# Chunk members made later, block fetches and row scatters placed earlier, a wider token row: one change to a fused attention and mixture-of-experts kernel

## The chip, the cores and the metric

The kernel runs on one core of a Trainium2 chip. The metric is the device time of one execution in microseconds (us), the median of the runs. A core has five engines that work side by side, each through its own instructions in order: TensorE (PE; its weight loads are listed apart as PEld), VectorE (DVE), ScalarE (ACT), GpSimd (POOL) and SyncE (SP). SP issues most of the transfers, POOL those that cast or go by an index.

## The reference

```python
ub = sum(maximum(q * k_min[chunk], q * k_max[chunk]), axis=-1)      # a bound for each chunk of 32 keys
top_chunks = argsort(where(causal, ub, -1e9))[..., -6:]             # six chunks for each query
scores = where(key in a top chunk and key <= query, q @ k.T / sqrt(D), -1e9)
x = (softmax(scores) @ v).transpose(0, 2, 1, 3).reshape(3072, 512)

y_dense = relu(x @ w1_dense) @ w2_dense
expert = argmax(x @ w_gate, axis=1)                                 # one of 8
y_moe[t] = gate_w[t] * (relu(x[t] @ w1[expert[t]]) @ w2[expert[t]])
out = y_dense + y_moe
```

There are 4 batches, 8 heads, 768 positions and a head size of 64.

## The kernel before

**Attention.** The 32 heads are worked off as 16 pairs (`NP`), four pairs to a batch; a pair has 11 units (`u`), each of one score tile (`scores`), its exponential on ACT (L558), in three of the 11 units a causal mask on POOL (L560), and one unit later the product with v (`av`, L573). A pair is prepared ahead: POOL casts k, q and v to 16 bits (`cast_qk`, `cast_v`), PE transposes them (`prep_k`, `prep_q`), ACT and DVE evict them, DVE reduces each chunk to its maximum and minimum (L496), PE makes the bounds (`prep_ub`, L527), DVE finds the six largest (L533) and the flags, and `prep_s` brings the flags into the upper or lower half of the queries' tile `rT`. The keys' tile `kT` carries beside the 64 numbers of a key the row of chunk members: `exf` has -30000 where a key is in a chunk and 0 elsewhere, made by two selects on POOL (L135, L137) and copied by `expand` into the six `kT` tiles on ACT (L145, L146). So one matmul gives the scores and shuts out what was not chosen.

**Dense part and routing.** When a batch's four pairs are done, `batch_fills` hangs its dense layers and its routing between the units of the next four pairs; the table `at` says at which unit: transposes (L267), gate, `ranks` (L296), and `place(t)` for six tiles of 128 tokens. `place` is an indirect transfer by POOL (L378) that scatters tokens into a table in HBM, sorted by expert. A row has the 512 numbers of x, the gate's weight and the token's number, `XW` = 528 elements of 2 bytes. `xbig` has two buffers, so the copy of the token numbers (L292, POOL) for a batch waits for the scatters of the batch two before.

**Expert part.** The table is worked off in blocks of 128 rows. `lists` makes each block's expert offset (`eo`) and row (`ro`); `load_rows` and `load_offs` bring them into registers of SP and PE through `registers` (L440, TENSOR_LOAD), `fetch` (L459) loads a block by its register, `tx` transposes it (L686), `e1` and `th` and `e2` are the two layers, and an indirect add (L715) sends the result to the output. The first `N1` = 11 blocks hold no token of the last batch, so they can be fetched before that batch is routed. 28 blocks run in the loop; three more run only if they are needed. `empty` writes zero rows behind each expert's tokens (L730).

**What sets the order.** The program's order is written out by hand, and a scheduler may move an instruction against its neighbours on an engine; each engine then works strictly in its order and waits on semaphores. SP's queue holds the loads, the stores of dense results (L408), the register loads and the fetches one behind the other. The token numbers' copy, the casts, the masks, the scatters and the weights' loads (`load_expert`, L207) share POOL's queue.

Of the kernel before, what the change touches and what calls it, by code (L numbers as in the profile page):

```python
# [12 lines left out]
ALU = mybir.AluOpType  # L13
# [4 lines left out]
def kernel(  # L18
# [22 lines left out]
    HP = H // 2  # L41
    NP = B * HP
    NBLK = NM + E - 1
    XW = Dm + 16
    U16 = mybir.dt.uint16

    const = ctx.enter_context(tc.tile_pool(name="const", bufs=1))
# [31 lines left out]
    def load(p, names="kqv"):  # L79
        if p >= NP:  # L80
            return
        b, hp = divmod(p, HP)
        for nm, src in (("k", k), ("q", q), ("v", v)):
            if nm not in names:
                continue
            f = aload.tile([128, 2, NT, D], FP, name=nm + "f")
            st[p][nm] = f
            for g in range(2):
                if nm == "v":
                    nc.sync.dma_start(out=f[:, g], in_=src[b, 2 * hp + g].rearrange("(t p) d -> p t d", p=128))  # L90
                else:
                    nc.sync.dma_start(out=f[:, g].rearrange("p (T j) d -> p T (j d)", j=NJ),
                                      in_=src[b, 2 * hp + g].rearrange("(T p j) d -> p T (j d)", p=128, j=NJ))
# [37 lines left out]
    for j in range(NJ):  # L131
        cb = cbias[64 * j : 64 * j + 64]
        nc.gpsimd.affine_select(out=cb, in_=cb, compare_op=ALU.is_ge,
                                fill=-60000.0, base=j, pattern=[[128, NT], [0, 2], [-32, NC]], channel_multiplier=2)
    nc.gpsimd.affine_select(out=exf[0:32], in_=exf[0:32], compare_op=ALU.is_ge, fill=0.0,  # L135
                            base=0, pattern=[[1, S]], channel_multiplier=-32)
    nc.gpsimd.affine_select(out=exf[0:32], in_=exf[0:32], compare_op=ALU.is_ge, fill=0.0,  # L137
                            base=31, pattern=[[-1, S]], channel_multiplier=32)
    for i in range(NB):
        nc.vector.memset(kT[i][0][64:128], 0.0)  # L140
        nc.vector.memset(kT[i][1][0:64], 0.0)
        nc.vector.memset(v16[i][:, :, :, D : D + 1], 1.0)

    def expand(i):
        nc.scalar.copy(kT[i][0][64:96, :], exf[0:32])  # L145
        nc.scalar.copy(kT[i][1][0:32, :], exf[0:32])  # L146
# [111 lines left out]
    def batch_fills(b):  # L258
# [111 lines left out]
        def place(t):  # L370

            def f():
                with tc.issue_after(latest["pool"].ins):
                    put(t)
            return f
# [51 lines left out]
            at.setdefault(n + n // NT, []).append(f)  # L427
        at.setdefault(9, []).append(ranks)
        for t in range(NT):
            at.setdefault(11 + 5 * t, []).append(place(t))  # L430
        U = HP * NU
        for n, f in enumerate(dense):
            at.setdefault(10 + n * (U - 12) // len(dense), []).append(f)
# [4 lines left out]

    def registers(src, engine, top, why):
        _, v = nc.values_load_multi_w_load_instructions(src, engines=[engine], min_val=0, max_val=top,  # L440
                                                        skip_runtime_bounds_check_because=why)
        return v

    def load_offs():
# [12 lines left out]
    def fetch(i):  # L457
        es[i]["x"] = xg = eg.tile([128, XW], U16, name="xg")
        ld = nc.sync.dma_start(out=xg, in_=table[bass.ds(rows[i], 128)])  # L459
        if i < N1:  # L460
            tc.add_to_no_dep_group("full", ld.ins)

    FIRST = 6
    with (
# [7 lines left out]
        def cast_qk(p):  # L472
            if p >= NP:
                return
            s = st[p]
            s["k16"] = k16 = ahead.tile([128, NT, 2, D], HF, name="k16")
            nc.gpsimd.tensor_copy(k16, s["k"].rearrange("p g t d -> p t g d"))  # L477
            s["q16"] = q16 = ahead.tile([128, NT, 2, D], HF, name="q16")
            nc.gpsimd.tensor_copy(q16, s["q"].rearrange("p g t d -> p t g d"))
# [39 lines left out]
        def prep_ub(p):  # L519

            s = st[p]
            ub = pprep.tile([128, NT, 2, NC], FP, name="pp")
            nc.tensor.matmul(ub.rearrange("p t g c -> p (t g c)"), ident, cbias.rearrange("p t g c -> p (t g c)"),
                             start=True, stop=False, skip_group_check=True)
            for t in range(NT):
                for n, (src, j) in enumerate(((s["qp"], 0), (s["qp"], 2), (rT[p % NB][0], 1))):
                    nc.tensor.matmul(ub[:, t].rearrange("p g c -> p (g c)"), src[:, t * 128 : (t + 1) * 128],  # L527
                                     s["kb"][:, j].rearrange("p g c -> p (g c)"),
                                     start=False, stop=(n == 2), skip_group_check=True)
            m = m8[p % 2]  # L530
            for t in range(1, NT):
                for g in range(2):
                    nc.vector.max(out=m[:, t, g], in_=ub[:, t, g, 0 : 4 * t + 4])  # L533
            flags = fl[p % 2].rearrange("p t (g c) -> p t g c", g=2)[:, :, :, 0:NC]
            nc.vector.tensor_tensor(flags, ub, m[:, :, :, 5:6].to_broadcast([128, NT, 2, NC]), ALU.is_lt)
# [50 lines left out]

        for kind in ("tr", "h", "y", "rk"):
            cur[kind] = (pfill, "fb")
        for i in range(NB):
            expand(i)  # L590
        cast_qk(0)
        load(2, "kq")
        prep_k(0)
        prep_q(0)
        prep_kt(0)
        cast_v(0)
        prep_ub(0)
        cast_qk(1)
        load(3, "kq")
        cast_v(1)  # L600
# [5 lines left out]
        prep_kt(1)  # L606
        cast_qk(2)
        load(4, "kq")
        prep_ub(1)

        wq = [(e, w) for e in range(E) for w in range(2)]
        ahead_n = 2
# [15 lines left out]
        for i, (p, u) in enumerate(seq):  # L628
            n1 = p + 1 if p + 1 < NP else None
            n2 = p + 2 if p + 2 < NP else None  # L630
            if i + ahead_n < len(seq):
                scores(*seq[i + ahead_n])
            if u == 2 and n1 is not None:
                prep_s(n1)
            if u == 4 and n2 is not None:
                prep_k(n2)
            if u == 5 and n2 is not None:
                prep_q(n2)
            if u == 7 and n2 is not None:
                prep_kt(n2)  # L640
            if u == 9 and n2 is not None:
                prep_ub(n2)
            for f in fills.pop(i % (HP * NU) - LAG, ()):
                f()
            if i >= LAG:
                finish(*seq[i - LAG])
            if u == 0 and n2 is not None:
                cast_v(n2)
                load(p + 4, "v")
                if p == 1:  # L650
                    load_dense(st[n2]["cast"])
                if p == 2:
                    route_consts()
                for _ in range(2 if p >= 10 else 1):
                    if p > 1 and wq:
                        load_expert(*wq.pop(0), st[n2]["cast"])
            if u == 7:
                cast_qk(p + 3)
                load(p + 5, "kq")
            if p == NP - 1 and u == 5:  # L660
                load_rows(N1)
                load_offs()
            if p == NP - 1 and u >= 5:
                fetch(u - 5)
        for i in range(len(seq) - LAG, len(seq)):
            finish(*seq[i])
        assert not wq
# [133 lines left out]
```

## Time and profile before

| | |
|---|---|
| median of 3 runs | 273.51 us (273.25 to 274.56) |
| the profiled execution: span, and its own time | 273.5 us, 275.16 us |
| busy: PE, DVE, ACT, POOL | 219.3 us (80%), 189.2 us (69%), 170.8 us (62%), 159.2 us (58%) |
| longest groups | exponentials (ACT, L558) 91.0 us; scores (PE, L554) 63.5 us; products with v (PE, L573) 45.7 us |
| transfers | 49.64 MB, mean 182 GB/s |
| granted clock of TensorE, mean | 0.985 |

The shares are means over stages of different kinds: attention up to about 179 us, with dense work hung in from the fifth pair on, then expert blocks with the last batch's dense part, and a tail of adds. Each stage has to be read by itself. A wait is told with the engine or transfer that ended it; a wait for several is put down to the last one.

### The profile page before, as it was taken

How to read it: one execution, taken by the hardware profiler on the slowest of the kernel's cores; microseconds unless marked ns; L12 is line 12 of the kernel's file. 1: busy time of each engine (PE TensorE's matmuls, PEld its weight loads, DVE VectorE, ACT ScalarE, POOL GpSimd, SP SyncE). 2: the span in 40 equal slices, each digit the busy share in tenths (PEclk: the TensorE clock that was granted, in tenths of full speed). 3: DMA queues.
4: the chain of work that ended last, by engine and by line, in shares of the span. 5: the costliest groups of instructions: out<-in, count | busy, mean ns of one | idle time of the engine just before them, and what ended most of it. 6: DMA issues, size and time to landing. Idle time of an engine off the chain costs nothing. (4 is left out here: it accounts for less than half of the span.)

```text
span 273.5 us, 7279 instructions
## 1 busy us (share of the span) xinstructions
PE 219.3 (80%) x2547; PEld 144.5 (53%) x2547; DVE 189.2 (69%) x587; ACT 170.8 (62%) x319; POOL 159.2 (58%) x197
## 2 busy tenths in 40 slices
PE   1159777888898968899995899939968999999970
PEld 0147565666565656656664666616524555555530
DVE  6288999999989759998797997216634345545540
ACT  2819979778669858668987568813424555555530
POOL 7565976546567656576827534400783445776662
PEclk9999999999999999999999999998999999999996
DMA  6999999998979989879996924256396999886875
GB/s 178 268 255 275 162 235 184 237 225 208 194 178 287 200 257 232 164 191 188 213 250 121 186 78 109 62 163 159 89 297 100 258 170 238 143 139 89 100 102 75
DMA packets 75108, 49.64 MB, mean 182 GB/s; under 512 B 29632, under 2 KB 68160, under 8 KB 75072
## 3 DMA queue, kind: packets, MB, share of 16 engines
q1 hardware_dynamic: 59856, 30.18, 43.7%
q0 software_dynamic: 15216, 18.99, 43.0%
q8 instruction: 21, 0.34, 0.5%
q14 instruction: 15, 0.12, 0.2%
HBM read 41.55 MB, written 18.09 MB: 218 GB/s over the span
## 5 line engine op out<-in xcount | busy, mean ns | idle before, releaser
L558 ACT ACTIVATE ex<-sp 128x512 f16<-128x512 f32 (+1 forms) x176 | 91.0, 595 | 17.7 <-PE sp L554 11.7
L554 PE MATMUL sp<-rT,kT 128*128 128x128 f16 (+3 forms) x384 | 63.5, 261 | 5.9 <-ACT ex L558 4.1
L715 POOL DMA_INDIRECT out_dram<-yo,xg x28 | 43.7, 1561 | 24.9 <-DVE yo L714 17.0
L573 PE MATMUL op<-v,ex 128*128 128x65 f16 x672 | 45.7, 194 | 6.5 <-POOL ex L560 5.3
L560 POOL TENSOR_SCALAR_AFFINE_SELECT ex<-ex 128x512 f16<-128x512 f16 x48 | 32.3, 678 | 31.3 <-ACT ex L558 28.9
L573 PEld LDWEIGHTS <-ex 128*128 128x128 f16 x672 | 35.8, 98 | 19.2 <-POOL ex L560 8.1
L378 POOL DMA_INDIRECT table<-xbig,slot x24 | 24.0, 999 | 26.3 <-DVE nf L334 15.4
L496 DVE TENSOR_REDUCE ks<-kp 128x24 f16<-128x768 f16 x32 | 29.2, 944 | 11.1 <-ACT kp L492 11.0
L554 PEld LDWEIGHTS <-kT 128*128 128x128 f16 x384 | 29.3, 98 | 13.2 <-issue 9.4
L714 DVE TENSOR_SCALAR yo<-yp,xg 128x512 f32<-128x512 f32 x28 | 21.0, 750 | 18.2 <-PE yp L711 12.2
L694 PE MATMUL hp<-we,exT 128*128 x112 | 30.0, 387 | 3.5 <-DMA xg<-table 1.8
L711 PE MATMUL yp<-we,ehT 128*128 x112 | 28.7, 379 | 2.2 <-ACT ys L239 1.3
L705 ACT COPY ehT<-tp 128x512 f16<-128x512 f16 x28 | 16.4, 586 | 22.2 <-PE tp L703 17.6
L688 DVE COPY exT<-tp 128x512 f16<-128x512 f16 x28 | 11.9, 424 | 24.2 <-PE tp L686 12.1
L393 PE MATMUL hp<-xT,wd 128*128 128x384 f16 x128 | 26.3, 325 | 2.6 <-DVE rt L310 1.0
L697 ACT ACTIVATE eh<-hp 128x512 f16<-128x512 f32 x28 | 16.7, 597 | 18.2 <-PE hp L694 15.0
L402 PE MATMUL yp<-wd,hT 128*128 128x512 f16 x96 | 24.8, 378 | 1.0 <-DVE ys L237 0.5
L395 ACT ACTIVATE hT<-hp 128x384 f16<-128x384 f32 x32 | 15.8, 494 | 12.0 <-PE hp L393 10.8
L492 ACT COPY kp<-pp 128x768 f16<-128x768 f16 x16 | 12.9, 804 | 10.7 <-PE pp L490 10.7
L477 POOL CAST k<-kf 128x768 f16<-128x768 f32 x16 | 13.2, 826 | 9.8 <-PE pp L490 7.8
L584 DVE TENSOR_TENSOR xbig<-op,rs 128x384 f16<-128x384 f32 x32 | 17.6, 551 | 0.5
L393 PEld LDWEIGHTS <-wd 128*128 128x128 f16 x128 | 11.8, 97 | 9.3 <-issue 5.0
(127 smaller groups left out, 391.9 us busy)
## 6 DMA issues: line engine op xcount, KB each, us to landing
we<-in_moe_w_dram POOLq DMA_DIRECT2D x16, 512.0 KB
kf<-in_k_dram SPq DMA_DIRECT2D x32, 192.0 KB
qf<-in_q_dram SPq DMA_DIRECT2D x32, 192.0 KB
vf<-in_v_dram SPq DMA_DIRECT2D x32, 192.0 KB
out_dram<-ys SPq DMA_DIRECT2D x48, 128.0 KB
xg<-table SPq DMA_DIRECT2D x28, 132.0 KB
table<-zt SPq DMA_DIRECT2D x9, 132.0 KB
wd<-in_moe_w_dense_dram POOLq DMA_DIRECT2D x2, 512.0 KB
```

What stands on the lines that cost most here:

```text
L378: sc = nc.gpsimd.indirect_dma_start(out=table, out_offset=bass.IndirectOffsetOnAxis(ap=keep["slot"][:, t : t + 1], axis=0), in_=xbig[b % 2 ...
L393: nc.tensor.matmul(hp, wd[:, ko, j * 128 : (j + 1) * 128], xT[:, ko, g * G * 128 : (g + 1) * G * 128], start=(ko == 0), stop=(ko == NK - 1))
L402: nc.tensor.matmul(yp, hold["h"][:, j, i * 128 : (i + 1) * 128], wd[:, NK + j], start=(j == 0), stop=(j == NK - 1))
L496: nc.vector.tensor_reduce(out=ks[:, i], in_=kp.rearrange("d (c w) -> d c w", w=32), op=op, axis=mybir.AxisListType.X)
L554: nc.tensor.matmul(sp[:, o : o + w], kT[p % NB][g][:, kt * 128 : (kt + 1) * 128], rT[p % NB][g][:, a * 128 : z * 128], start=(o == 0), sto ...
L558: nc.scalar.activation(ex[:, 0:o], sp[:, 0:o], AF.Exp, scale=0.125)
L560: latest["pool"] = nc.gpsimd.affine_select(out=ex, in_=ex, compare_op=ALU.is_ge, fill=0.0, base=0, pattern=[[0, 4], [1, 2], [2, 64]], chan ...
L573: nc.tensor.matmul(s["op", g][:, t * (D + 1) : (t + 1) * (D + 1)], ex[:, o : o + 128], v16[p % NB][:, g, kt, :], start=first, stop=(last_o ...
L694: nc.tensor.matmul(hp, s["xT"][:, ko], wef[:, bass.ds(offs[i] + ko * 512, 512)], start=(ko == 0), stop=(ko == NK - 1))
L711: nc.tensor.matmul(yp, s["hT"][:, j], wef[:, bass.ds(offs[i] + (NK + j) * 512, 512)], start=(j == 0), stop=(j == NK - 1))
L714: nc.vector.tensor_scalar(o, yp, s["x"][:, Dm : Dm + 2].bitcast(FP), None, ALU.mult)
L715: sc = nc.gpsimd.indirect_dma_start(out=out, out_offset=bass.IndirectOffsetOnAxis(ap=s["x"][:, Dm + 2 : Dm + 4].bitcast(mybir.dt.int32), a ...
```

## The change

Four edits. The selects that make `exf` become a function `members`, called after the first `cast_qk`; `expand` is called for pair 0 behind that pair's bounds and for 1 and 2 behind pair 1's. `place(t)` comes every fourth unit, not every fifth. `load_rows` and `load_offs` are called in the last pair but one, at unit 8, and the first fetches from unit 3 of the last pair, not 5; the register loads may no longer be moved by the builder (`bass_reorder=False`). The token row has 544 elements, 1088 bytes, not 528, 1056 bytes.

```diff
-    XW = Dm + 16
+    XW = Dm + 32
...
-    nc.gpsimd.affine_select(out=exf[0:32], in_=exf[0:32], compare_op=ALU.is_ge, fill=0.0,
-                            base=0, pattern=[[1, S]], channel_multiplier=-32)
-    nc.gpsimd.affine_select(out=exf[0:32], in_=exf[0:32], compare_op=ALU.is_ge, fill=0.0,
-                            base=31, pattern=[[-1, S]], channel_multiplier=32)
...
+    def members():
+        nc.gpsimd.affine_select(out=exf[0:32], in_=exf[0:32], compare_op=ALU.is_ge, fill=0.0,
+                                base=0, pattern=[[1, S]], channel_multiplier=-32)
+        nc.gpsimd.affine_select(out=exf[0:32], in_=exf[0:32], compare_op=ALU.is_ge, fill=0.0,
+                                base=31, pattern=[[-1, S]], channel_multiplier=32)
...
         for t in range(NT):
-            at.setdefault(11 + 5 * t, []).append(place(t))
+            at.setdefault(11 + 4 * t, []).append(place(t))
...
         _, v = nc.values_load_multi_w_load_instructions(src, engines=[engine], min_val=0, max_val=top,
-                                                        skip_runtime_bounds_check_because=why)
+                                                        skip_runtime_bounds_check_because=why,
+                                                        bass_reorder=False)
...
-        for i in range(NB):
-            expand(i)
         cast_qk(0)
+        members()
         load(2, "kq")
         prep_k(0)
         prep_q(0)
         prep_kt(0)
         cast_v(0)
         prep_ub(0)
+        expand(0)
         cast_qk(1)
...
         load(4, "kq")
+        expand(1)
         prep_ub(1)
+        expand(2)
...
-            if p == NP - 1 and u == 5:
+            if p == NP - 2 and u == 8:
                 load_rows(N1)
                 load_offs()
-            if p == NP - 1 and u >= 5:
-                fetch(u - 5)
+            if p == NP - 1 and 3 <= u < 3 + FIRST:
+                fetch(u - 3)
```

How the order moves, at three places. First the start on ACT, where `kp` and `qp` are pair 0's keys and queries; before:

```order
L145 ACT_TABLE_LOAD
L145 COPY kT_0_105<-exf 32x768
L146 COPY kT_1_106<-exf 32x768
L145 COPY kT_0_107<-exf 32x768
L146 COPY kT_1_108<-exf 32x768
L145 COPY kT_0_109<-exf 32x768
L146 COPY kT_1_110<-exf 32x768
L492 COPY kp<-pp 128x768
L516 ACTIVATE qp<-pp 128x768
```

And now:

```order
L495 ACT_TABLE_LOAD
L495 COPY kp<-pp 128x768
L519 ACTIVATE qp<-pp 128x768
L147 COPY kT_0_105<-exf 32x768
L148 COPY kT_1_106<-exf 32x768
L147 COPY kT_0_107<-exf 32x768
L148 COPY kT_1_108<-exf 32x768
L147 COPY kT_0_109<-exf 32x768
L148 COPY kT_1_110<-exf 32x768
```

All six copies of the members stand behind pair 0's two evictions, not ahead of them. In the same stage POOL's last steps up to the first mask are now these (`v_2` is pair 2's v, `k_494` are pair 3's keys, L563 is the mask):

```order
L189 MEMSET zt 128x1
L294 COPY xbig_171<-num 128x6
L294 COPY xbig_172<-num 128x6
L480 CAST k_494<-kf 128x768
L487 CAST v_2_119<-vf 128x12x64
L563 AFFINE_SELECT ex<-ex 128x512
```

Pair 2's v and pair 3's keys have changed places; both casts still stand ahead of the first mask. Second, POOL around the copy of the token numbers in pairs 7 and 8, from a scatter (DMA table) to that copy; before:

```order
L378 DMA table<-xbig_173,slot 25728x528
L484 CAST v_0_117<-vf 128x12x64
L207 DMA we<-in_moe_w_dram 128x4x512
L560 AFFINE_SELECT ex<-ex 128x512
L477 CAST k_2296<-kf 128x768
L560 AFFINE_SELECT ex<-ex 128x512
L378 DMA table<-xbig_173,slot 25728x528
L479 CAST q_2298<-qf 128x768
L292 COPY xbig_173<-num 128x6
L560 AFFINE_SELECT ex<-ex 128x512
```

And now:

```order
L380 DMA table<-xbig_171,slot 25728x544
L487 CAST v_0_117<-vf 128x12x64
L209 DMA we<-in_moe_w_dram 128x4x512
L563 AFFINE_SELECT ex<-ex 128x512
L294 COPY xbig_171<-num 128x6
L480 CAST k_2296<-kf 128x768
L563 AFFINE_SELECT ex<-ex 128x512
```

The scatter at the top was the batch's fifth and is now its sixth and last; the sixth stood behind the weights' load and one place ahead of a cast and the copy. Third, SP's queue in the last two pairs, from the register load of the block rows on; before:

```order
L408 DMA out_dram<-ys 64x512 x14
L440 TENSOR_LOAD ro
L459 ISA
L459 DMA xg<-table 128x528
L408 DMA out_dram<-ys 64x512 x2
```

And now:

```order
L410 DMA out_dram<-ys 64x512 x6
L442 TENSOR_LOAD ro
L410 DMA out_dram<-ys 64x512 x6
L462 ISA
L462 DMA xg<-table 128x544
L462 ISA
L462 DMA xg<-table 128x544
```

The register load is eight stores earlier, and the first seven fetches stand together, two stores earlier than the first one stood. On PE the first register load of expert offsets likewise moves from between `tx(0)` and `e1(0)` into pair 14, and the second from block 4 to ahead of `tx(0)`.

## Rows read from the trace of the kernel before

**Rows 1.** Busy time by stretch: PE, PEld, DVE, ACT, POOL; clock, DMA share, GB/s.

```profile
20.00:40.00 20.00, 16.50 (x250) 11.96 (x249) 18.57 (x56) 17.62 (x34) 14.93 (x20) 1.00 1.11 219
60.00:80.00 20.00, 18.03 (x255) 12.67 (x253) 19.09 (x67) 13.42 (x26) 12.21 (x15) 1.00 0.86 205
...
220.00:240.00 20.00, 20.00 (x145) 11.13 (x144) 10.50 (x18) 10.64 (x18) 12.39 (x8) 1.00 0.93 181
240.00:260.00 20.00, 19.67 (x145) 10.97 (x143) 10.58 (x18) 10.63 (x18) 14.05 (x10) 1.00 0.77 107
```

**Rows 2.** Timeline of the start: start, duration, engine, line, operation, count, idle before.

```profile
6.30 0.83 ACT L145 COPY kT<-exf 32x768 f16<-32x768 f16 x1 [1.09 <-POOL exf L137]
...
11.30 0.78 ACT L492 COPY kp<-pp 128x768 f16<-128x768 f16 x1
```

**Rows 3.** Timeline of POOL, 14 to 26 us, to the first mask.

```profile
19.91 0.83 POOL L484 CAST v<-vf 128x768 f16<-128x768 f32 x1 [1.22 <-DMA vf<-in_v_dram]
...
21.45 0.67 POOL L560 TENSOR_SCALAR_AFFINE_SELECT ex<-ex 128x512 f16<-128x512 f16 x1
```

**Rows 4.** Timeline, 22 to 25 us: two weight loads of the same kind, and DVE.

```profile
22.18 0.32 PEld L573 LDWEIGHTS <-ex 128*128 128x128 f16 x4
...
23.90 0.21 PEld L573 LDWEIGHTS <-ex 128*128 128x128 f16 x4
...
24.12 0.91 DVE L533 MAX8 m<-pp 128x8 f32<-128x8 f32 x10
```

**Rows 5.** Timeline of POOL, 82 to 101 us: scatters, a weights' load, the numbers' copy.

```profile
88.78 0.81 POOL L207 DMA_DIRECT2D we<-in_moe_w_dram  x1
...
92.70 1.01 POOL L378 DMA_INDIRECT table<-xbig,slot  x1 [0.16 <-issue]
...
98.82 0.26 POOL L292 COPY xbig<-num 128x6 int32<-128x6 int32 x1 [4.27 <-DMA table<-xbig,slot]
```

**Rows 6.** Timeline around both copies: PE behind them, and POOL at the second.

```profile
99.74 0.30 PE L573 MATMUL op<-v,ex 128*128 128x65 f16 x4 [2.19 <-POOL ex L560]
...
143.75 0.20 POOL L292 COPY xbig<-num 128x6 int32<-128x6 int32 x1 [4.77 <-DMA out_dram<-ys]
...
146.91 0.20 PE L573 MATMUL op<-v,ex 128*128 128x65 f16 x1 [1.99 <-POOL ex L560]
```

**Rows 7.** Timeline of the passage from attention to the blocks: POOL, SP, PE, DVE.

```profile
170.70 0.97 POOL L378 DMA_INDIRECT table<-xbig,slot  x1 [0.16 <-issue]
...
175.85 0.97 POOL L378 DMA_INDIRECT table<-xbig,slot  x1 [0.16 <-issue]
...
178.73 0.34 PEld L573 LDWEIGHTS <-ex 128*128 128x128 f16 x3
...
179.60 0.37 SPq L459 DMA_DIRECT2D xg<-table  x1
...
181.65 0.40 PE L686 MATMUL tp<-ident,xg 128*128 128x128 f16 x4 [2.45 <-DMA xg<-table]
...
182.58 0.55 DVE L584 TENSOR_TENSOR xbig<-op,rs 128x384 f16<-128x384 f32 x1
...
183.88 1.86 PE L694 MATMUL hp<-we,exT 128*128 x4 [1.83 <-DMA xg<-table]
```

**Rows 8.** Busy time by stretch, columns as in rows 1, the first block's.

```profile
184.00:186.00 2.00, 2.00 (x9) 0.90 (x8) 0.00 (x0) 0.17 (x1) 0.00 (x0) 0.50 0.91 204
```

**Rows 9.** Register loads of L440: count, ns min/median/max, first and last start.

```profile
L440 PEldq TENSOR_LOAD <-eo x8: 329/436/777, 183.2 to 261.0; - x8
L440 SPq TENSOR_LOAD <-ro x2: 1967/4058/6148, 177.4 to 202.9; - x2
```

**Rows 10.** Timeline of block 4, the first layer on PE.

```profile
201.75 1.02 PE L694 MATMUL hp<-we,exT 128*128 x4 [1.26 <-DVE ys L237]
```

**Rows 11.** DMA queue q1, 4 to 24 and 184 to 188.5 us: packets, MB, share.

```profile
q1 hardware_dynamic: 14198, 5.25, 123.5%
...
q1 hardware_dynamic: 998, 1.05, 91.9%
```

## The prediction

> **What bounds the kernel now.** I read the busy times by stretch first, then the timeline where an engine other than the busiest one sets the pace. In the first pairs the reader is to see VectorE at 18.6 and 19.1 of 20 us: there an instruction fewer ahead of DVE counts, a faster transfer doesn't. In the blocks it is TensorE, at 20.0 and 19.7 of 20 us [rows 1]. So time is to be had where these engines stand still, and the timeline shows four such places: the start, two copies of token numbers on POOL, the passage from attention to the blocks, and block 4. The transfers' share is 0.77 to 1.11 [rows 1], but it isn't the limit in the blocks, where PE has no gap.
>
> **The start.** Pair 0's keys are evicted on ACT at 11.30 us only, since six copies of the members, 0.83 us each, begin at 6.30 ahead of it [rows 2]. The change puts them behind: 6 x 0.83 = 5.0 us (11.30 - 6.30) off pair 0's path. What is late next decides. Every product with v needs its mask from POOL, and on POOL the first mask (21.45) stands behind the cast of pair 2's v, which waits until 19.91 for its transfer [rows 3]. That queue is full all the while, at 123.5% of the 16 engines over 4 to 24 us [rows 11], so v lands no sooner. In the new order pair 3's keys are cast ahead of this v instead of behind it, one cast, as long as that of v, in POOL's idle time: the mask starts at 19.91 + 0.83 = 20.74, that is 0.71 sooner. PE, in order, stands before the first product until then, and with it pair 1's bounds and DVE's search at 24.12 [rows 4]. PE has done its early scores by then and stands idle, which has a price: the same four weight loads took 0.32 us at 22.18 and 0.21 at 23.90 [rows 4], so TensorE came from 1.2 to 2.4 GHz in between, while it worked without a break, and now that work breaks off. Some 2 us more at 1.2 GHz would cost about 1 us of PE's progress, of which DVE, fed ahead, feels part. I take a gain of **0.7 us**, near the row on the mask; the ends are a loss of 1.0 and, if neither v nor the mask held it, the 5.0. The selects for `exf` themselves cost nothing: they fill POOL's waits for pair 0's v and are needed by ACT only after `qp`.
>
> **Scatters every fourth unit.** The copy of token numbers into `xbig` waits for the six scatters of the batch two before. The last one is issued at 92.70, behind a weights' load of 88.78 in the same queue, and the copy starts at 98.82 after 4.27 us of waiting [rows 5]; the second time at 143.75 after 4.77 [rows 6]. Behind the copy on POOL stands a mask, behind the mask PE: 2.19 and 1.99 us [rows 6], together 4.2. Now the last scatter takes the place of the fifth, ahead of the load of 88.78 and about 2 us before it. From issue to completion the scatter of 92.70 took some 6 us with that load ahead of it (98.82 - 92.70); without it I use the bound of the passage below, 3.75 us, so it is done by about 90.5, when POOL, behind the load's 0.81 and a mask, comes to the copy. The second time the scatter goes to the place of a former fifth one, over 5 us ahead of its copy. Each scatter costs POOL the same 1 us as before. I take **4.0 us** of the 4.2; the ends are 0 (the copies still wait) and 4.2 (PE's two gaps). DVE and ACT idle in the same gaps, so nothing else is late at once.
>
> **Fetches and register loads.** The last scatter of the third batch is issued at 175.85, the first fetch at 179.60, PE's transposes of it start at 181.65 after 2.45 us, and the first layer of block 0 at 183.88 [rows 7]. SP's register load ran from 177.4 for 1.97 us [rows 9], right ahead of the fetch; so the scatter was done within 3.75 us of its issue. Now the scatter takes the place of 170.70 [rows 7] and is done by 174.5; the register load is past, and block 0 has landed by about 177 (from issue to PE's start it took 181.65 - 179.60 = 2.05). PE's last products with v are loaded at 178.73 [rows 7], so `tx(0)` and `tx(1)` run from about 179.3, 0.4 each. The next limit is DVE: its eviction of block 0, 0.42, and the last normalization, 0.55 at 182.58 [rows 7], end at about 180.7, and `e1(0)` starts at 180.9: 3.0 us sooner. Then the clock: after that idle stretch it stood at 0.50, 1.2 GHz, from 184 to 186 [rows 8], and block 0's four matmuls took 1.86 us [rows 7] where block 4's took 1.02 [rows 10]: 0.84. With one gap under 2 us, where there were 2.45 and 1.83 with 0.4 of work between, I expect no fall. `tx(1)` has moved out of the way as well, some 0.2. Sum **4.0 us**; the ends are 2.0, the register load alone, and 5.1, from 178.73 to 183.88 without any wait. What SP's queue is moved past: two stores wait behind seven fetches, at 0.5 us each 3.5 us later at most; `ys` has three buffers and PE made one in about 2 us there, so I cost it at nothing, and at up to 1 us if that cover is gone.
>
> On PE the eight register loads take 0.33 to 0.78 us each [rows 9]. Block 4's stood right ahead of matmuls that came after 1.26 us of idle time [rows 10]; it moves ahead of `tx(0)`. Two loads now stand in the stream of the last two pairs, 0.66 to 1.56 us together, where work in flight covers part. Net gain **0.5 us**, between -0.3 and 1.26. The Trainium skill, DMA: Bandwidth & Descriptors, Latency and other measured facts, gives a floor of about 0.6 us for such a load. By it I estimate 1.2 us for the two, a net gain of nearly nothing and a sum of 0.5 us less; the trace has loads of 0.33 us, so the row decides. SP's second load, 6.1 us [rows 9], now stands ahead of a store, which has its buffer to itself; cost nothing.
>
> **The wider row.** 32 bytes more on 28 fetches, 9 zero writes and 24 scatters. A packet of 370 bytes on average took 1.235 x 16 x 20 us / 14198 = 28 ns, one of the fetches' stretch 0.919 x 16 x 4.5 / 998 = 66 ns [rows 11]: by their slope, 38 ns over 690 bytes, 32 bytes cost under 2 ns, and 61 x 128 / 16 x 2 ns is 1 us of transfer time off PE's path. I take 0; between a loss of 1 and a gain of 1, as rows can't show what alignment gives.
>
> **Sum.** 0.7 + 4.0 + 4.0 + 0.5 = 9.2 us off the profiled execution: its span 273.5 to 264.3, its time 275.16 to 266.0. That execution lay 1.65 us above the median of 273.51, so the median goes to **264.3**.
>
> **Rivals.** (a) *The start counts in full.* For it speaks that DVE, the busiest engine of this stage, cannot begin on pair 0 before the eviction at 11.30; against it the mask. It gives 4.3 more: 260.0. (b) *The copies still wait*: the scatter lands behind another load, and POOL stops at the copy, which is now ahead of one more cast. For it speaks the same queue, shared with the weights' loads; against it the order. It gives 273.5 - 5.2 = 268.3. (c) *Slower: the blocks become bound by transfers.* The share there is 0.93 and 0.77 [rows 1], which leaves 0.07 x 20 + 0.23 x 20 = 6 us. If a wider packet cost 150 ns instead of 66, the fetches' 28 x 128 / 16 packets per engine would add 84 ns x 224 = 18.8 us, 12.8 after the 6, and 273.5 - 9.2 + 12.8 = 277.1. From 133 ns on it eats the whole gain (15.2 us). Against it speaks the slope above. (d) *The start's break in PE's work, SP's longer blocks and the queue cancel the gains*, each taking its lower end: -1.0 + 0 + 2.0 + 0 - 1 - 1 = -1.0 of gain: 274.5, no change within 0.5%.
>
> **How the numbers follow.** Forecast 0.60, (a) 0.08, (b) 0.18, (c) 0.05, (d) 0.09. The likeliest gives 264.3. Its own ends with not all terms at once reach from 262 to 267. The range takes in (a) and (b), with something above (b) for a start at its lower end (268.3 + 0.7 + 1.0 = 270.0): 259.5 to 270.0. It leaves out (c) and (d), 0.14, and a little more for what I haven't seen. Over 0.5% (1.4 us, about what a measurement of this kernel can tell from no change) faster are the forecast, (a) and (b), 0.86; within it (d), 0.09; slower (c), 0.05.
>
> **What would show it.** At the start: the first key eviction at about 6.5 us, and the first mask at about 20.7, right behind the cast of v; a mask at 16 or 17 would speak for (a). At the copies: no wait over 1 us on POOL and no gap of 2 us on PE; a wait of 4 us for (b). At the passage: fetches issued at about 170 us on the new time scale, all before attention ends, `e1(0)` within 2 us of the last product with v, and no stretch at 0.50. In the blocks: PE at 20 of 20 us and row packets within 2 ns; gaps on PE that a fetch ends would speak for (c). I am wrong above all if PE's gaps come back at other instructions, since each gain here is a gap taken away, not work.

## The result and the profile after

The changed kernel takes 262.26 us (median of 4, 262.05 to 262.42); the kernel before, measured beside it, 273.38. The ratio is 0.9607, with a 95% interval of 0.9533 to 0.9681. (Here and below the ratio is estimated from the runs, and differs a little from the quotient of two medians.) Forecast were 264.3 us, 259.5 to 270.0. The profiled execution has a span of 260.5 us, 13.0 less than that of before, and its time is the median; that of before lay 1.65 us above its median, so the spans overstate the gain by about that.

Busy time by stretch of the changed kernel, columns as in [rows 1]:

```profile
20.00:40.00 20.00, 15.48 (x225) 11.99 (x226) 14.04 (x47) 14.97 (x28) 14.02 (x19) 0.83 1.01 194
60.00:80.00 20.00, 18.04 (x255) 12.67 (x252) 19.30 (x68) 13.42 (x26) 13.05 (x16) 1.00 0.93 221
...
180.00:200.00 20.00, 19.85 (x159) 11.19 (x156) 11.31 (x38) 10.47 (x20) 13.76 (x11) 1.00 0.65 153
```

The limits are those of before, VectorE in the pairs and TensorE in the blocks. Two stretches differ. In 20 to 40 us VectorE is busy for 14.04 us where it was 18.57 [rows 1], at a granted clock of 0.83: a new hole. The 1.00 of [rows 1] doesn't mean that the kernel before had no slow stretch there: by its weight loads, 0.32 us and then 0.21, TensorE came to full speed only between 22.18 and 23.90 us [rows 4]. In 180 to 200 us TensorE is busy throughout.

**The start**, by the timelines of ACT, POOL, PE and DVE, answering to [rows 2 to 4]:

```profile
6.63 0.80 ACT L495 COPY kp<-pp 128x768 f16<-128x768 f16 x1 [4.53 <-PE pp L493]
```

```profile
19.68 0.96 POOL L487 CAST v<-vf 128x768 f16<-128x768 f32 x1 [0.22 <-DMA vf<-in_v_dram]
20.59 0.66 POOL L563 TENSOR_SCALAR_AFFINE_SELECT ex<-ex 128x512 f16<-128x512 f16 x1
```

```profile
21.30 0.40 PE L576 MATMUL op<-v,ex 128*128 128x65 f16 x4 [4.01 <-POOL ex L563]
```

```profile
23.44 0.91 DVE L536 MAX8 m<-pp 128x8 f32<-128x8 f32 x10 [3.49 <-PE pp L530]
```

and the busy times of single microseconds in it:

```profile
20.00:21.00 1.00, 0.00 (x0) 0.00 (x0) 0.00 (x0) 0.00 (x0) 1.00 (x2) 0.50 1.20 244
...
25.00:26.00 1.00, 1.00 (x13) 0.77 (x12) 0.76 (x3) 0.89 (x3) 0.25 (x1) 0.50 1.15 276
27.00:28.00 1.00, 0.90 (x20) 0.80 (x18) 0.83 (x2) 0.52 (x1) 0.49 (x1) 1.00 0.58 153
```

The first key eviction is 4.67 us sooner, the first mask only 0.86, since it stands behind the cast of pair 2's v. PE waits 4.01 us for it, the granted clock falls to 0.50 (1.2 GHz), and it is still there in the microsecond at 25. VectorE's search for pair 1 begins 0.68 us sooner, at 23.44, but pair 1's first exponential comes 0.50 us later (the table below).

**The copies of token numbers and the passage**, answering to [rows 5 to 7, 10], by the timelines of POOL, SP and PE:

```profile
86.89 0.98 POOL L380 DMA_INDIRECT table<-xbig,slot  x1 [0.17 <-issue]
...
88.90 0.79 POOL L209 DMA_DIRECT2D we<-in_moe_w_dram  x1
...
92.94 0.19 POOL L294 COPY xbig<-num 128x6 int32<-128x6 int32 x1 [1.83 <-DMA table<-xbig,slot]
...
135.05 0.19 POOL L294 COPY xbig<-num 128x6 int32<-128x6 int32 x1
...
166.25 0.97 POOL L380 DMA_INDIRECT table<-xbig,slot  x1 [0.16 <-issue]
```

```profile
168.71 3.89 SPq L462 DMA_DIRECT2D xg<-table  x7
```

```profile
94.56 0.30 PE L576 MATMUL op<-v,ex 128*128 128x65 f16 x4 [1.16 <-POOL ex L563]
...
174.48 0.26 PE L576 MATMUL op<-v,ex 128*128 128x65 f16 x3
174.58 0.61 PE L691 MATMUL tp<-ident,xg 128*128 128x128 f16 x8
176.18 1.02 PE L699 MATMUL hp<-we,exT 128*128 x4 [0.99 <-DVE xbig L587]
...
189.76 1.03 PE L699 MATMUL hp<-we,exT 128*128 x4
```

POOL's waits of 4.27 and 4.77 us are down to 1.83 and nothing, and PE's gaps behind them from 2.19 and 1.99 [rows 6] to 1.16 and nothing. Seven fetches are out before attention ends; `tx(0)` and `tx(1)` follow the last product at once, and one gap of 0.99 us is left where 2.45 and 1.83 stood. The row at 189.76 is block 4's first layer: the gap of 1.26 us [rows 10] is not there.

Where along the program the time went can be read off two things that both kernels do once at each place, the first exponential of a pair on ACT and the first layer of a block on PE. Their starts, and the ends of the spans, in us:

| | before | after | difference |
|---|---|---|---|
| pair 0, first exponential | 20.20 | 15.69 | -4.51 |
| pair 1 | 27.73 | 28.23 | +0.50 |
| pair 7 | 85.19 | 85.39 | +0.20 |
| pair 10 | 117.57 | 115.91 | -1.66 |
| pair 15, last exponential | 177.63 | 173.17 | -4.46 |
| block 0 | 183.88 | 176.18 | -7.70 |
| block 3 | 196.29 | 186.72 | -9.57 |
| block 5 | 207.15 | 193.66 | -13.49 |
| block 27 | 261.50 | 248.35 | -13.15 |
| end of span | 273.5 | 260.5 | -13.0 |

So the start lost 0.2, the copies gave 4.7, the passage up to block 3 gave 5.1, and blocks 3 to 5 gave 3.9, where 0.5 was forecast. The start and blocks 3 to 5 needed experiments.

### The profile page after: what moved, and what is told of

The parts are those of the page before. It is cut to its first block, busy times and chain, and to the rows that moved or that the text cites. A ratio compares the mean times of both kernels' runs of the same rounds, so it can differ in the third digit from the quotient of the medians.

```text
span 260.5 us, 7277 instructions
## 1 busy us (share of the span) xinstructions
PE 217.9 (84%) x2547; PEld 144.6 (55%) x2547; DVE 188.1 (72%) x587; ACT 171.3 (66%) x319; POOL 159.1 (61%) x197
## 5 line engine op out<-in xcount | busy, mean ns | idle before, releaser
L557 PE MATMUL sp<-rT,kT 128*128 128x128 f16 (+3 forms) x384 | 64.7, 265 | 5.4 <-ACT ex L561 3.6
L576 PE MATMUL op<-v,ex 128*128 128x65 f16 x672 | 46.4, 196 | 7.3 <-POOL ex L563 6.3
L563 POOL TENSOR_SCALAR_AFFINE_SELECT ex<-ex 128x512 f16<-128x512 f16 x48 | 32.4, 679 | 32.2 <-ACT ex L561 28.9
L576 PEld LDWEIGHTS <-ex 128*128 128x128 f16 x672 | 36.7, 100 | 20.0 <-POOL ex L563 8.6
L699 PE MATMUL hp<-we,exT 128*128 x112 | 29.1, 379 | 1.0 <-DVE xbig L587 1.0
L536 DVE MAX8 m<-pp 128x8 f32<-128x8 f32 (+4 forms) x160 | 16.2, 167 | 3.7 <-PE pp L530 3.5
```

The lines of the kernel that those rows point to most:

```text
L557: nc.tensor.matmul(sp[:, o : o + w], kT[p % NB][g][:, kt * 128 : (kt + 1) * 128], rT[p % NB][g][:, a * 128 : z * 128], start=(o == 0), sto ...
L563: latest["pool"] = nc.gpsimd.affine_select(out=ex, in_=ex, compare_op=ALU.is_ge, fill=0.0, base=0, pattern=[[0, 4], [1, 2], [2, 64]], chan ...
L576: nc.tensor.matmul(s["op", g][:, t * (D + 1) : (t + 1) * (D + 1)], ex[:, o : o + 128], v16[p % NB][:, g, kt, :], start=first, stop=(last_o ...
L699: nc.tensor.matmul(hp, s["xT"][:, ko], wef[:, bass.ds(offs[i] + ko * 512, 512)], start=(ko == 0), stop=(ko == NK - 1))
```

## The experiments

**One part at a time.** Four kernels, each with one part of the change alone, ran on one chip.

The start alone (b_start; the copies `expand(0)` to `expand(2)` also go where the change has them):

```diff
-        for i in range(NB):
-            expand(i)
         cast_qk(0)
+        members()
```

The scatters alone (b_place):

```diff
-            at.setdefault(11 + 5 * t, []).append(place(t))
+            at.setdefault(11 + 4 * t, []).append(place(t))
```

The register loads and fetches alone (b_fetch):

```diff
-            if p == NP - 1 and u == 5:
+            if p == NP - 2 and u == 8:
                 load_rows(N1)
                 load_offs()
-            if p == NP - 1 and u >= 5:
-                fetch(u - 5)
+            if p == NP - 1 and 3 <= u < 3 + FIRST:
+                fetch(u - 3)
...
+                                                        bass_reorder=False)
```

The row alone (b_row):

```diff
-    XW = Dm + 16
+    XW = Dm + 32
```

> The kernel before with the start alone: members behind the first pair's casts, the six copies spread out. Theory (the first mask, behind the cast of pair 2's v, holds PE, and TensorE then stays at 1.2 GHz longer): first key eviction at about 6.6 us, first mask at about 20.6, granted clock 0.50 from 20 to 26 us, attention no earlier than before: between 1.0 us faster and 0.5 slower than 273.4. Rival (the start counts in full): 4 to 5 us faster, about 269.

> The kernel before with the scatters at every fourth unit alone. Theory: both waits of POOL at the numbers' copy go, with PE's gaps of 2.19 and 1.99 us behind them: 4.2 to 4.6 us faster, about 269, with PE's three gaps around block 4 (3.4 us together) still there. Rival (those gaps are an accident of when things meet, and any shift of the blocks removes them): 7.5 to 8 us faster, about 265.5. Rival (a gap taken away comes back at another instruction): under 2 us faster.

> The kernel before with the earlier register loads and fetches alone (the register loads also keep the place they are written at). Theory: attention ends as before, the passage loses 4 to 5 us and its stretch at 1.2 GHz goes; if the three gaps around block 4 (3.4 us) came from the register load that stood there on PE, they go too: 8 to 8.9 us faster, about 265. Rival (the gaps come from the row's size or from anything else): 4 to 5 us faster, about 269, with the gaps still there.

> The kernel before with the wider row alone (1088 bytes for 1056). Theory: nothing, within 1 us of 273.4, and the gaps around block 4 stay. Rival (rows that begin at odd multiples of 32 bytes slow the zero writes, scatters and fetches, and the gaps around block 4 come from that): the gaps of 3.4 us go, 3 to 4 us faster, about 270.

Measured, against 276.40 us of the kernel before on that chip (273.28 to 279.43, 29 runs):

| | median | ratio to before, 95% interval |
|---|---|---|
| b_start | 277.67 | 1.0049 (1.0008 to 1.0091) |
| b_place | 266.53 | 0.9667 (0.9619 to 0.9716) |
| b_fetch | 275.32 | 0.9946 (0.9896 to 0.9997) |
| b_row | 276.75 | 1.0024 (0.9983 to 1.0066) |

The scatters alone gave 9.9 us, more than any expectation; the fetches alone 1.1, less than any. In the passage both have the same ground. The timelines of POOL, SP and PE of b_fetch show what a fetch waits for:

```profile
173.33 0.97 POOL L378 DMA_INDIRECT table<-xbig,slot  x1 [0.16 <-issue]
...
178.67 0.96 POOL L378 DMA_INDIRECT table<-xbig,slot  x1 [0.35 <-issue]
```

```profile
175.79 0.37 SPq L460 DMA_DIRECT2D xg<-table  x1
...
182.14 0.36 SPq L460 DMA_DIRECT2D xg<-table  x1
```

```profile
181.66 0.39 PE L687 MATMUL tp<-ident,xg 128*128 128x128 f16 x4
184.26 0.40 PE L687 MATMUL tp<-ident,xg 128*128 128x128 f16 x4 [2.22 <-DMA xg<-table]
186.03 1.44 PE L695 MATMUL hp<-we,exT 128*128 x3 [1.37 <-DMA xg<-table]
```

The program asks for the fetches earlier, but each waits for the scatters ahead of it in the program. The first leaves 2.46 us after the fifth scatter's issue (175.79 - 173.33), and `tx(0)` follows the last product at once. The second leaves only 3.47 us after the last scatter's issue (182.14 - 178.67), and behind it PE waits 2.22 us for `tx(1)`, which stands ahead of `e1(0)`: a fetch moved ahead of what it depends on gains little. With the scatters early and the fetches as before (b_place), seven fetches already leave before the last exponential at 175.03:

```profile
170.57 3.89 SPq L459 DMA_DIRECT2D xg<-table  x7
```

The passage, from the last exponential to the first layer of block 0, took 3.67 us there (175.03 to 178.70), where before it took 6.25 and in the changed kernel 3.01. The row's width gave nothing that can be told. b_start measured 1.3 us slower, but a repeat of the kernel before, below, differed from itself by more. Its trace has the first mask at 20.51 and half the clock at 22, as the first theory said, and pair 3 begins at 43.88 us, 0.2 to 0.4 sooner than in the three others on that chip.

**Parts taken out of the change.** Three kernels on another chip, where the kernel before took 274.58 us: the changed kernel with the start of before, with the row of before, and with register loads that the scheduler may move.

```diff
+        for i in range(NB):
+            expand(i)
         cast_qk(0)
-        members()
...
-    XW = Dm + 32
+    XW = Dm + 16
...
-                                                        bass_reorder=False)
```

> The changed kernel with the start as it was before: members and all six copies first. Theory (the start is worth nothing, since the mask behind the cast of pair 2's v gates it): ratio to the kernel before 0.955 to 0.963, the same as the changed kernel's 0.9607 or 1 us better, no half clock after 23 us, no gaps around block 4. Rival (the start counts in full, 4 to 5 us): 0.976 or more. Rival for the gaps around block 4 (they went because the whole program shifted): they come back, 2 to 3.5 us, ratio 0.968 to 0.973.

> The changed kernel with the narrower row of before (1056 bytes). Theory (the row costs and gives nothing): ratio 0.957 to 0.964, no gaps around block 4. Rival (with the scatters and fetches early, the row's alignment is what keeps the blocks free of gaps): the gaps around block 4 come back, 2 to 3.5 us, ratio 0.968 to 0.973.

> The changed kernel, with the register loads free to be moved by the scheduler as before. Theory A (the gaps around block 4 come from PE's register load that stood there): that load is back ahead of block 4, and gaps of 1 to 3.4 us with it, ratio 0.965 to 0.973. Theory B (they come from the fetches and scatters of the first blocks still running then, not from the load): at most the load's own 0.5 to 1 us, ratio 0.961 to 0.964.

Measured: 262.07 us for a_nostart (ratio 0.9612, 0.9511 to 0.9713), 261.73 for a_norow (0.9545, 0.9460 to 0.9630), 263.74 for a_noreorder (0.9624, 0.9553 to 0.9695). All three intervals overlap that of the change: neither start nor row can be told from nothing. Pair 7 begins at 85.19 us with the start of before (a_nostart), and at 85.92 and 85.39 with the new one (a_norow, a_noreorder). In none do PE's gaps around block 4 come back; in a_noreorder a register load of 1.11 us starts at 190.61, right ahead of block 4 at 192.07, without a gap, so theory A on the register load falls. The load does show elsewhere: in a_noreorder one stands between the last product and block 0, where PE waits 1.63 us for 0.99 in the changed kernel, 0.64 us.

```profile
178.30 1.02 PE L698 MATMUL hp<-we,exT 128*128 x4 [1.63 <-DVE exT L692]
```

**The gaps around block 4, both kernels on one chip.** The kernel before and the changed one ran once more, unedited, on a third chip, and with them the scatters and fetches together without anything else of the change.

> The kernel before once more, to have its trace from the same chip as the changed kernel's. Theory A (the gaps of PE around block 4, 3.4 us, with PE's completions reported up to 3 us late, belong to this kernel): they are there, 2 to 3.6 us, while the changed kernel has none. Theory B (they belong to the chip or to the execution): both kernels have them or neither has.

> The changed kernel once more, on the same chip as the three others of this call. Ratio to the kernel before 0.953 to 0.968, as first measured; theory A: no gap of PE over 0.5 us from block 1 to block 8; theory B: the same gaps as in the kernel before on this chip.

> The kernel before with the scatters at every fourth unit and the earlier register loads and fetches, and nothing else: no change of the start, of the row or of what may move a register load. Theory (these two are the change; the fetches are worth nothing until the scatters are out of their way): alone they gave 9.9 us and 1.1 us, together 11 to 12.5 us, ratio 0.955 to 0.962, within 1 us of the changed kernel. Rival (keeping the register loads in their place is worth what the run without it lacked, 1 to 2 us): ratio 0.962 to 0.966, slower than the changed kernel by that.

Measured: before_again 276.38 us, after_again 262.77 (0.9618, 0.9579 to 0.9657), b_place_fetch 262.73 (0.9624, 0.9581 to 0.9666); the ratios are to the first load of the kernel before on this chip, 272.65 us. By time, the scatters and the fetches are the whole change. The traces say how it divides. `e1(0)` of b_place_fetch:

```profile
177.25 1.02 PE L694 MATMUL hp<-we,exT 128*128 x4 [1.61 <-DVE exT L688]
```

That is 3.63 us after the last exponential (173.62), hardly less than the 3.67 of b_place: once the scatters are early, calling the fetches early adds nothing up to block 0, and 0.4 us up to block 3 (14.17 us for 14.56). The step from there to 3.01 is the register load ahead of `e1(0)`: a_noreorder, which differs from the changed kernel in nothing else, takes 3.64. Of the 4.0 us by which b_place's span is longer than the changed kernel's, 2.5 are gaps around block 4, which its trace has: 9.45 us from block 3 to block 5, where traces without gaps have 6.94.

The timeline of PE in before_again, around block 4:

```profile
201.60 1.03 PE L711 MATMUL yp<-we,ehT 128*128 x4
202.46 0.39 PE L703 MATMUL tp<-ident,eh 128*128 128x128 f16 x4
202.69 1.03 PE L694 MATMUL hp<-we,exT 128*128 x4
203.55 0.39 PE L686 MATMUL tp<-ident,xg 128*128 128x128 f16 x4
203.77 1.89 PE L402 MATMUL yp<-wd,hT 128*128 128x512 f16 x8
205.50 1.03 PE L711 MATMUL yp<-we,ehT 128*128 x4
```

and the same place in the kernel before, from the trace that the prediction used:

```profile
200.09 0.40 PE L703 MATMUL tp<-ident,eh 128*128 128x128 f16 x4 [0.83 <-PE yp L711]
...
206.07 0.59 PE L711 MATMUL yp<-we,ehT 128*128 x2 [1.34 <-ACT ys L239]
```

Same kernel, same order, no gap: theory B. The gaps belong to an execution or a chip, not to what the change took away. What made them is open. They were in the first trace of before and in the four of one-part kernels, all with PE's completions seen by ACT and VectorE up to 3 us late; b_fetch, with its register load far ahead, and b_row, with the wider row, had them too.

In this pair of traces from one chip the terms are free of these gaps. Starts in us:

| | before_again | after_again | difference |
|---|---|---|---|
| pair 7, first exponential | 85.20 | 85.05 | -0.15 |
| pair 15, last exponential | 179.97 | 174.58 | -5.39 |
| block 3 | 199.65 | 188.13 | -11.52 |
| block 5 | 206.59 | 195.06 | -11.53 |
| end of span | 273.9 | 260.4 | -13.5 |

The copies wait 4.22 and 5.69 us in before_again, and the passage runs at half the clock for longer than in [rows 8]. PE's waits behind the two copies, 2.19 and 2.91 us, are followed by half the clock too (the first two of the stretches below), which the trace of before doesn't have.

```profile
145.94 0.19 POOL L292 COPY xbig<-num 128x6 int32<-128x6 int32 x1 [5.69 <-DMA table<-xbig,slot]
```

```profile
100.00:102.00 2.00, 2.00 (x26) 1.86 (x24) 0.00 (x0) 1.23 (x3) 1.35 (x3) 0.50 0.34 102
152.00:154.00 2.00, 2.00 (x29) 1.94 (x28) 1.21 (x5) 1.67 (x4) 2.00 (x3) 0.50 1.26 214
...
186.00:188.00 2.00, 1.69 (x5) 0.59 (x5) 0.00 (x0) 0.00 (x0) 0.00 (x0) 0.50 0.80 167
188.00:190.00 2.00, 1.91 (x15) 1.47 (x14) 1.11 (x3) 0.60 (x1) 0.00 (x0) 0.50 1.04 272
```

The first of these stretches in the trace of before, with 42 matmuls for 26:

```profile
100.00:102.00 2.00, 2.00 (x42) 1.87 (x39) 0.34 (x1) 1.70 (x4) 1.87 (x4) 1.00 0.32 85
```

Such a stretch lengthens a pair by over 1 us: pair 8 takes 11.61 us here and 10.35 in the trace of before. after_again has one as well, at 0.50 from 152 to 154 us, and its pair 13 takes 13.17 us, against 11.81 in the changed kernel's first trace. So a term of one pair of traces is good to no better than that.

**Giving the start back its 4 us.** If the first mask's place on POOL holds the start, moving it should free it. The first try moves the mask alone; the second also keeps the casts that wait for transfers behind all three masks of pair 0, and puts the routing constants into POOL's wait.

```diff
             if u == 0 and n2 is not None:
-                cast_v(n2)
+                with tc.issue_after(first["mask"].ins):
+                    cast_v(n2)
...
-                    route_consts()
+                    with tc.issue_after(first["mask"].ins):
+                        route_consts()
...
-                cast_qk(p + 3)
+                with tc.issue_after(first["mask"].ins):
+                    cast_qk(p + 3)
```

The second try differs from it for pair 0:

```diff
+            if i == 5:
+                with tc.issue_after(masks[-1].ins):
+                    cast_v(2)
+                load(4, "v")
...
+                with tc.issue_after(masks[-1].ins if p == 0 else masks[0].ins):
+                    cast_qk(p + 3)
```

> The changed kernel with POOL's first mask ahead of the cast of pair 2's v, of pair 3's casts and of the routing constants. Theory (the mask alone held the start): first mask at about 16.5 to 17 us instead of 20.6, PE's wait of 4 us before its first product with v goes, TensorE stays at 2.4 GHz from 20 to 26 us, attention ends 3 to 4.5 us sooner: ratio 0.945 to 0.951. Rival (what is behind the mask, pair 2's v or DVE's share of 0.93 to 0.97 in these pairs, holds it next): under 1.5 us, 0.956 to 0.961.

> The changed kernel with the routing constants in POOL's wait behind the first mask, and the cast of pair 2's v and the casts of pair 3 behind all three masks of pair 0. Theory (POOL's place in line alone held the start; the run with only the first mask moved lost what it gained at the second and third, which stood behind the same cast): masks at about 16.2, 20.9 and 21.6 us, no gap of PE over 2 us from 17 to 26 us, pair 1's first exponential at 25 to 26 us instead of 28.2, and the program 2 to 3.5 us faster than the changed kernel. Rival (transfers hold the first pairs: the queue of the inputs is full until 27 us, so pair 2 starts no sooner): pair 2 begins within 0.7 us of the changed kernel's 36.5, and the program is within 1 us of it. Rival (PE's break brings 1.2 GHz back): pair 1 no sooner than 27.5.

a_mask, beside the three kernels of the second group, took 265.22 us (0.9666, 0.9578 to 0.9753): a miss. It is the highest median of the four, though the intervals overlap, and pair 2 begins 1.11 us later than in the changed kernel (37.61 for 36.50). Its timelines of POOL and PE, and its clock:

```profile
16.18 0.67 POOL L564 TENSOR_SCALAR_AFFINE_SELECT ex<-ex 128x512 f16<-128x512 f16 x1 [0.32 <-ACT ex L562]
19.57 0.83 POOL L488 CAST v<-vf 128x768 f16<-128x768 f32 x1 [2.73 <-DMA vf<-in_v_dram]
...
23.19 0.66 POOL L564 TENSOR_SCALAR_AFFINE_SELECT ex<-ex 128x512 f16<-128x512 f16 x1
```

```profile
23.91 0.40 PE L578 MATMUL op<-v,ex 128*128 128x65 f16 x4 [4.06 <-POOL ex L564]
```

```profile
28.00:29.00 1.00, 1.00 (x9) 0.63 (x7) 0.67 (x2) 0.82 (x2) 0.51 (x1) 0.50 0.08 24
```

The first mask is 4.4 us sooner and the second stands behind the same cast and the constants: PE's wait of 4 us has only moved, and half the clock with it, to 29 us. a_mask2 took 260.70 us (259.48 to 262.37; 0.9562, 0.9514 to 0.9610), 2.1 less than after_again's 262.77 (261.27 to 263.12) on the same chip. The ranges of the six runs each overlap at their edges, so the size is less sure than the sign. By its trace:

```profile
20.05 1.29 POOL L564 TENSOR_SCALAR_AFFINE_SELECT ex<-ex 128x512 f16<-128x512 f16 x2
...
27.95 1.08 POOL L202 DMA_DIRECT2D wg<-in_moe_w_gate_dram  x1 [1.85 <-issue]
29.04 0.80 POOL L203 DMA_DIRECT2D wd<-in_moe_w_dense_dram  x1
29.83 0.74 POOL L204 DMA_DIRECT2D wd<-in_moe_w_dense_dram  x1
30.59 1.29 POOL L564 TENSOR_SCALAR_AFFINE_SELECT ex<-ex 128x512 f16<-128x512 f16 x2
```

```profile
31.32 0.40 PE L578 MATMUL op<-v,ex 128*128 128x65 f16 x4 [2.17 <-POOL ex L564]
```

Pair 1's first exponential comes at 23.46 us, 3.98 sooner than in after_again, and pair 2's at 34.30, 1.86 sooner, so transfers do not hold it where it was. From there the lead stays near 2 us as far as pair 12. Half of it is lost again at one place: pair 1's masks stand behind three issues of dense weights on POOL, 2.62 us, the first after 1.85 us of idle time. So POOL's order held the start. That it holds what is left too was not tested, since the dense weights were not moved. This kernel has the lowest median measured here.

## Why the prediction was right

The time, 262.26 for 264.3, is inside the range, and the likeliest case came: the copies and the passage carry the gain, the start gives next to nothing. By its terms, in us, against the two pairs of traces:

| term | forecast | first traces | one chip |
|---|---|---|---|
| start (to pair 7) | 0.7 | -0.2 | 0.15 |
| copies (pair 7 to the last exponential) | 4.0 | 4.7 | 5.2 |
| passage (to block 3) | 4.0 | 5.1 | 6.1 |
| register loads (blocks 3 to 5) | 0.5 | 3.9 | 0.0 |
| the rest, to the end | 0 | -0.5 | 2.0 |
| sum | 9.2 | 13.0 | 13.5 |

- **The start**: the mechanism held, the mask at 20.59 for 20.74, and rival (a), the start in full, fell for the reason given. Mis-sized is its price: "some 2 us more at 1.2 GHz would cost about 1 us". The granted clock was at 0.50 in the microseconds at 20 and 25 and back at 1.00 by 27, 2 to 5 us after TensorE came to full speed in before [rows 4]. Pair 1 began 0.50 us later (0.08 on one chip), not sooner.
- **The copies**: at the second copy the wait and PE's gap went, as forecast; at the first a wait of 1.83 us was left, where none over 1 us was forecast, and a gap of 1.16 on PE. The step on the scatter's duration failed: "without it I use the bound of the passage below, 3.75 us". It took 6.05 us (86.89 to 92.94) with the load behind it instead of ahead; the place a unit sooner made up for most of that. What made it long is not shown: the load is one candidate, the other transfers another, for all together were at 1.13 of the 16 engines then, and at 0.39 when the scatter of 166.25 took 2.46 us (up to the fetch of 168.71; rows below). PE's two gaps shrank by 3.0 us together in the first traces, less than the 4.0 forecast; the term measured 4.7 and 5.2, over its upper end of 4.2. PE's idle time from pair 7 to the last exponential fell by more than that, from 11.7 us to 7.6 in all, and the waits of before are not fixed: 4.27 and 4.77 us in the trace used, 4.22 and 5.69 in before_again. What the forecast left out here is the clock: in before_again each of PE's two gaps is followed by a stretch at 0.50; in the trace used neither is.
- **The passage**: `e1(0)` starts 1.7 us after the last product with v is issued at 174.48, at full clock, as forecast ("within 2 us"). The term was worth 5.1 to 6.1 instead of 4.0; the low term is the clock's, 0.84 for the four matmuls of block 0 alone: from block 0 to block 3 before took 12.41 us and the changed kernel 10.54. In before_again it stood at 0.50 from 186 to 190 us, so transposes behind those matmuls were slow as well. The two parts that were priced together are not alike: the early fetch alone is worth 1.1 us, and with the scatters out of its way 0.4 at most by the traces (b_place and b_place_fetch). The scatters carry the passage.
- **The register loads**: the 0.5 rests on the gap of 1.26 us ahead of block 4, "block 4's stood right ahead of matmuls that came after 1.26 us of idle time". That reading was wrong: before_again has the same order of instructions and no gap. What keeping them in place is worth is 0.64 us, at block 0, and stands in the table under the passage. The Trainium skill, DMA: Bandwidth & Descriptors, Latency and other measured facts, has a floor of about 0.6 us for such a load; the trace does not agree, with a shortest one of 0.33 us (the group of PE's register loads below), and its median is 0.62.
- **The wider row**: nothing that can be told, by b_row, a_norow and b_place_fetch. Of rival (b) the wait of 1.83 us came; (c) and (d) did not.
- **The rest**: 2.0 us on one chip, some 0.9 of it between block 5 and block 27, was not forecast, and its cause is open.

The stretches of two scatters in the changed kernel, columns as in [rows 1]:

```profile
86.89:92.70 5.81, 5.54 (x72) 3.73 (x68) 3.67 (x18) 5.07 (x11) 3.23 (x4) 1.00 1.13 277
166.25:168.70 2.45, 2.34 (x30) 1.61 (x29) 0.75 (x2) 2.04 (x6) 0.97 (x1) 1.00 0.39 115
```

PE's register loads of the changed kernel, columns as in [rows 9]:

```profile
L442 PEldq TENSOR_LOAD <-eo x8: 329/620/1204, 160.4 to 243.0; - x8
```

The sum came close partly by luck. On one chip the copies and the passage gave 3.3 us more than forecast and the rest 2.0, the start and the register loads some 1 less; and the forecast was taken from a trace 1.65 us above its median. That trace held some 3.4 us of gaps that are not the kernel's. before_again, without them, is as long (a span of 273.9 us for 273.5), having lost some 3.4 us more between pair 7 and block 3, where it ran at half the clock more often.

## What to carry to other kernels

A transfer asked for sooner moves only if what it depends on has moved too: find the last writer's completion, and price the two as one. In an engine that takes its work in order, one instruction that waits for a transfer holds all that is behind it; moving a single victim ahead only shows the next one, so move the waiting instruction behind every one of them. Take a second trace of the kernel before, best on the chip of the changed one, ahead of putting a price on a gap: one that a repeat doesn't have is no term of the sum, and one that both have can be followed by half the clock in only one of them.

## What was not expected of the hardware

- The same kernel, loaded a second time on one chip, measured 1.0119 of its first load (1.0068 to 1.0171; 276.38 and 272.65 us). That is more than b_start or b_row moved it. The mean granted clock of a run was 0.961 to 0.964 in the second load and 0.951 to 0.985 in the first. The changed kernel's runs lay within 0.4 us in its first measurement and within 1.9 in its second.
- Waits of PE of 4.01, 4.06 and 2.17 us in the first pairs were each followed by microseconds at a granted clock of 0.50, in most of which PE had work all the time: the wait is paid a second time. A wait of 2.19 us at the first copy was followed by it in before_again and not in the trace of before.
- A scatter of 128 rows took 2.46 and 3.47 us from issue to the fetch that waits for it, with nothing else issued in its queue (b_fetch, 173.33 to 175.79 and 178.67 to 182.14), and 6.05 us to the copy that waits for it where the transfers were at 1.13 of the engines (86.89 to 92.94 in the changed kernel).
- In some executions ACT and VectorE saw PE's completions up to 3 us late for some 10 us, with no wait in PE's own rows that would explain it. It came with five traces, on two occasions, and not with the other nine; neither the register load nor the row's width made it, and its cause is open.
